# Values of an attention kernel on four quarters of TensorE's array, three score tiles, gathers a step further ahead

## The chip, the cores and the metric

The kernel runs on one core of one Trainium2 chip. The metric is the device time of one execution in microseconds (us). Three executions of the kernel before took 1350.11, 1344.72 and 1342.0 us; their median is 1344.72.

## The reference

Talking-heads attention for 4 batches, 12 heads, 448 positions and 64 channels per head, and behind it two MLPs (768 to 2048 to 768) on all 1792 tokens:

```python
scores = np.matmul(q, k.transpose(0, 1, 3, 2)) / np.sqrt(64)
scores = np.einsum('bhij,hg->bgij', scores, w_pre)      # mixes the heads ("pre mix")
attn = softmax(scores)                                  # over j, with 1e-9 in the divisor
attn = np.einsum('bhij,hg->bgij', attn, w_post)         # mixes the heads again ("post mix")
x = np.matmul(attn, v)                                  # values; then tokens x 768
h = x @ moe_w_in;   x = np.where(h > 0, h, np.exp(np.minimum(h, 0)) - 1) @ moe_w_out
h = x @ moe2_w_in;  out = np.maximum(h, 0) ** 2 @ moe2_w_out
```

## The kernel before, in words

The diff touches the attention stage and the plan that starts the MLPs beside its end; the MLPs themselves (from about 436 us on) keep their order.

**Tiling.** The 448 rows of a batch are cut into groups of 10 rows, and the groups into four chunks of 12, 11, 11 and 11 groups. There are 16 chunks (4 batches) and 180 groups. Two groups make a step: T = 90 steps. In memory a partition of a score tile holds one pair of (row of a group, head), so that one matmul can mix heads.

**The stages.** `scores(n, p)` (L141 to L151) makes the scores of heads p and p + 6 of chunk n in two PSUM banks; it uses four quarters (64 x 64) of the array at once, and there are six such pairs per chunk. `keep_scores` copies the banks to the chunk's score tile `sc[n]`. `gather(s)` (L161 to L168) fetches the 120 lines of each of the two groups of step s from the score tile to a tile `graw`, with two DMAs per group, so four per step. `mix_pre(s)` mixes heads (L176), `maxima(s)` finds the maxima on VectorE (L184) and the exponentials on ScalarE (L186), `weigh(s)` makes the weights with the divisor, `mix_post(s)` (L210) mixes again and turns the tile, `keep_weighed` (L225; L222 and L223 in the last steps) copies the result to `at[n]`. `values(n, i)` (L229 to L242) multiplies by v for two heads: each matmul contracts 112 positions and fills 64 output channels, so it uses one half of the array, and two run beside each other. Six such calls make a chunk; the first three fill one "pv" bank, the last three fill it again. `keep_x` (L247) copies a full bank, `store_x` (L254) stores it to DRAM two steps later.

**The order.** It is written out by hand: each engine and each queue works in program order. In step s the loop at its end issues weigh(s + 1), at most one pair of scores, gather(s + AHEAD) with AHEAD = 4, mix_pre and maxima of step s + 2, the stores, mix_post(s), the values of the step, further scores, keep_x, and then loads. `put` fills the table of what is done beside which step: pairs of scores of chunk n between the last gather of chunk n - 2 and the first of chunk n (two score tiles take turns), query loads four steps before, values in the five steps behind a chunk's last group, the step with the fewest scores taking two. All DMAs of the stage go through the sync queue (SP) but a few at the very start: gathers, key tiles `kt` (L120), query tiles `qt` (L129), values `v` (L136), stores `xd` (L254), and near the end tokens for the first MLP, `tmp` (L620), and weights (L407, L503). Of `graw` there are eight tiles, so a gather can be issued when the pre mix of four steps before is done.

**PSUM and the end.** Of the eight banks three are "qk" (scores), two "mix", two "post" and one "pv". `Mlps.plan` closes the pools of keys, queries and one score tile at step `last` (`start`) and opens the pools `xp` and `tp` in their space; `load_x` fills `tmp` tiles in `tp`, `split_x` splits them.

Of the kernel before, what the change touches and what calls it, by code (L numbers as in the profile page):

```python
# [45 lines left out]
BANKS = {"qk": 3, "mix": 2, "post": 2, "pv": 1}  # L46
# [6 lines left out]
def attention(tc, dram, psum, qr, kr, vr, w_pre, w_post, diagonal, xd, mlps):  # L53
# [6 lines left out]
    with ExitStack() as ctx:  # L60
        work = ctx.enter_context(tc.tile_pool(name="work", bufs=1, side="left"))
        score_ctx = [ctx.enter_context(ExitStack()) for _ in range(2)]
# [4 lines left out]
        AHEAD, MIX, LATE = 4, 2, 2  # L67
# [71 lines left out]
        sc, taken, weighed, summed, stored = {}, [], [], [], []  # L139

        def scores(n, p, tags=("qk", "qk")):  # L141

            if p == 0:
                sc[n] = score[(n + 1) % 2].tile([128, H, S], F32, name="sc", bufs=1)
            k = kt[chunks[n][0]]
            out = [bank(psum, tag)[:, :S] for tag in tags]
            for c, (x, y) in enumerate(QROWS):
                for a in range(2):
                    o = slice(64 * a, 64 * a + 64)
                    nc.tensor.matmul(out[a][64 * c : 64 * c + 64], qt[n][o, p, x:y], k[o, p, :], start=True, stop=True)  # L150
            taken.extend((sc[n][:, 6 * a + p, :], out[a]) for a in range(2))  # L151
# [9 lines left out]
        def gather(s):  # L161
            for t in (2 * s, 2 * s + 1):
                n, g = groups[t]
                x = work.tile([128, S], F32, name="graw", bufs=2 * (AHEAD - MIX + 2))
                for r in range(2):
                    lines = slice(SROWS[r] + g, SROWS[r] + g + (R5 - 1) * H + 1, H)
                    nc.sync.dma_start(out=x[64 * r : 64 * r + HALF], in_=sc[n][lines])
                graw[t] = x  # L168
# [10 lines left out]
        def maxima(s):  # L179
            tot[s] = work.tile([128, 2], F32, name="tot", bufs=3)  # L180
            ex[s] = []
            for r, p in enumerate(mixed.pop(s)):
                nmax = work.tile([128, 1], F32, name="nmax", bufs=4)
                nc.vector.tensor_reduce(nmax, p, AX.X, ALU.max, negate=True)  # L184
                e = work.tile([128, S], F32, name="ex", bufs=2 * (MIX + 2))
                nc.scalar.activation(e, p, AF.Exp, bias=nmax, scale=1.0, accum_out=tot[s][:, r : r + 1])  # L186
                ex[s].append(e)
# [40 lines left out]
        def values(n, i):  # L228
# [3 lines left out]
            if i % 3 == 0:  # L232
                pv[n] = bank(psum, "post" if n == N - 1 and i else "pv")[:, : 3 * CH].rearrange("p (k i) -> p k i", k=3)
            for jc in range(JC):
                for g in (2 * i, 2 * i + 1):
                    o = 64 * (g % 2)
                    nc.tensor.matmul(  # L237
                        pv[n][o : o + 64, i % 3, :w], vt[b, i // 3][:, jc, g % 6 * D : (g % 6 + 1) * D], at[n][:, jc, g, :w],
                        start=(jc == 0), stop=(jc == JC - 1),
                    )  # L240
            if i % 3 == 2:
                summed.append((xd[b][:, i - 2 : i + 1, r0 : r0 + w], pv[n][:, :, :w]))  # L242

        def keep_x(s):
            for o, p in summed:
                x = work.tile([128, 3, CH], F32, name="xs", bufs=3)[:, :, : o.shape[2]]
                nc.scalar.copy(x, p)  # L247
                stored.append((s + LATE, o, x))
            summed.clear()
# [12 lines left out]
        work_at = [0] * (T + 8)  # L262
# [10 lines left out]
        for n in range(N):  # L273
# [3 lines left out]
            steps = sorted(steps + [min(steps, key=lambda x: work_at[x])])  # L277
# [9 lines left out]
        idle = work.tile([128, 512], mybir.dt.bfloat16, name="idle", tag="ex", bufs=2 * (MIX + 2))  # L287
# [7 lines left out]
        tags = ("qk", "qk"), ("mix", "mix"), ("post", "post"), ("qk", "pv")  # L295
# [7 lines left out]
        load_q(1, 0, 4)  # L303
        load_mixes()
        load_q(1, 4, 6)
        for n in range(2):
            for p in range(4 if n else 6):
                scores(n, p, tags[(6 * n + p) % 4] if n == 0 else ("qk", "qk"))
                keep_scores((act, dve))
                if n and p % 2:  # L310
                    mix_pre(p // 2)
                    maxima(p // 2)
            if n == 0:
                prepare_mixes()
                for s in range(AHEAD):
                    gather(s)
        weigh(0)
        for p in range(2):
            put(p, scores, 1, 4 + p)
# [30 lines left out]
        keep_x(T)  # L350
# [188 lines left out]
class Mlps:  # L539
# [474 lines left out]
```

## Time and profile before

| | us |
|---|---|
| median of three runs | 1344.72 |
| the profiled execution | 1345.77 |
| its span, first to last instruction | 1344.0 |
| TensorE busy in the span | 1301.3 (97%) |
| VectorE, ScalarE busy | 939.0 (70%), 687.1 (51%) |
| attention stage, to the first matmul of the MLPs | about 436 |

The sums below are made on the profiled execution, whose span lies 1.8 us under its own time. Matmuls are pipelined, and one that waits for its operand counts as busy, so a busy TensorE need not be one at its peak. The sync queue has no busy share on the page: it issues only, and what it does is read from its timeline.

### The profile page before, as it was taken

How to read it: one execution, taken by the hardware profiler on the slowest of the kernel's cores; microseconds unless marked ns; L12 is line 12 of the kernel's file. 1: busy time of each engine (PE TensorE's matmuls, PEld its weight loads, DVE VectorE, ACT ScalarE, POOL GpSimd, SP SyncE). 2: the span in 40 equal slices, each digit the busy share in tenths (PEclk: the TensorE clock that was granted, in tenths of full speed). 3: DMA queues.
4: the chain of work that ended last, by engine and by line, in shares of the span. 5: the costliest groups of instructions: out<-in, count | busy, mean ns of one | idle time of the engine just before them, and what ended most of it. 6: DMA issues, size and time to landing. Idle time of an engine off the chain costs nothing.

```text
span 1344.0 us, 33493 instructions
## 1 busy us (share of the span) xinstructions
PE 1301.3 (97%) x13456; PEld 1105.0 (82%) x13456; DVE 939.0 (70%) x1944; ACT 687.1 (51%) x1478; POOL 48.8 (4%) x110
## 2 busy tenths in 40 slices
PE   7899999999999999999989999999999999999998
PEld 3556566556567999998889999999999998999998
DVE  4556556547474899877789998767885548887452
ACT  4456556546563677433344454546664535445342
POOL 0001000001022000000000000000000000000000
PEclk9999999989999999999989999999999999999999
DMA  4544544554453555465666654513122120222131
GB/s 136 161 158 152 168 151 145 167 156 153 166 176 113 184 177 165 149 186 175 199 226 218 213 198 142 182 61 97 50 65 72 54 70 25 71 65 71 42 100 41
DMA packets 121662, 178.14 MB, mean 133 GB/s; under 512 B 24259, under 2 KB 99875, under 8 KB 121507
## 3 DMA queue, kind: packets, MB, share of 16 engines
q1 hardware_dynamic: 121266, 175.71, 41.0%
q8 instruction: 106, 1.74, 0.5%
q14 instruction: 50, 0.40, 0.1%
q10 hardware_dynamic: 240, 0.29, 0.1%
HBM read 101.07 MB, written 36.18 MB: 102 GB/s over the span
## 4 chain that ended last, share of the span: by engine, by line
PE 77%; DMA 11%; DVE 6%; ACT 3%; SPq 2%; issue 1%; POOL 0%; ACTq 0%; POOLq 0%
DMA graw<-sc 8%; PE ps_qk L635 8%; PE ps_qk L636 8%; PE ps_qk L637 8%; PE ps_mix L176 5%; PE ps_post L635 5%; PE ps_post L637 5%; PE ps_post L636 5%; PE ps_post L210 5%; PE ps_mix L637 5%; PE ps_mix L636 5%; PE ps_mix L635 5%; PE ps_qk L150 4%; PE ps_pv L237 4%; PE ps_pv L636 2%; PE ps_pv L637 2%
## 5 line engine op out<-in xcount | busy, mean ns | idle before, releaser
L490 ACT CAST wh<-wf 128x384 fp32r<-128x384 f32 (+1 forms) x272 | 133.2, 491 | 214.5 <-DVE wf L449 129.8
L497 DVE TENSOR_TENSOR wl<-wf,wh 128x384 fp32r<-128x384 f32 (+1 forms) x272 | 143.5, 530 | 78.9 <-ACT wh L490 77.2
L184 DVE TENSOR_REDUCE nmax<-ps_mix 128x1 f32<-128x448 f32 x180 | 106.2, 620 | 128.1 <-PE ps_mix L176 126.0
L176 PE MATMUL ps_mix<-graw,pre 60*64 60x448 f32 x720 | 144.1, 558 | 17.0 <-DMA graw<-sc 12.9
L186 ACT ACTIVATE ex<-ps_mix,nmax 128x448 f32<-128x448 f32 x180 | 112.9, 632 | 91.9 <-DVE nmax L184 91.0
L210 PEld LDWEIGHTS ps_post<-wg,ex 60*48 60x48 f32 (+1 forms) x5760 | 116.2, 129 | 33.6 <-issue 30.5
L641 DVE TENSOR_TENSOR rl<-hr,rh 128x896 fp32r<-128x896 f32 x96 | 104.5, 1089 | 54.1 <-ACT rh L640 54.1
L155 ACT COPY sc<-ps_qk 128x448 f32<-128x448 f32 x179 | 87.0, 539 | 88.1 <-PE ps_qk L150 34.0
L150 PE MATMUL ps_qk<-kt,qt 64*64 64x448 f32 x740 | 111.4, 572 | 12.1 <-ACT sc L155 8.6
L210 PE MATMUL ps_post<-wg,ex 60*64 60x60 f32 (+1 forms) x5760 | 119.1, 219 | 0.2 <-issue 0.2
L640 ACT CAST rh<-hr 128x896 fp32r<-128x896 f32 x96 | 90.0, 938 | 50.3 <-PE ps_post L637 25.1
L176 PEld LDWEIGHTS ps_mix<-graw,pre 60*64 60x64 f32 x720 | 40.5, 136 | 87.2 <-DMA graw<-sc 39.1
L225 DVE COPY at<-ps_post 112x480 f32<-112x480 f32 x174 | 105.7, 649 | 6.9 <-PE ps_post L210 6.8
L237 PE MATMUL ps_pv<-at,v 112*64 112x110 f32 (+2 forms) x1488 | 89.6, 267 | 0.0
L419 ACT ACTIVATE wf<-wd 128x384 f32<-128x384 f32 (+1 forms) x134 | 68.0, 512 | 38.6 <-DMA wd<-w1o 23.4
L635 PE MATMUL ps_qk<-xh,wh 128*128 128x448 f32 x216 | 79.3, 367 | 0.0
L636 PE MATMUL ps_qk<-xl,wh 128*128 128x448 f32 x216 | 79.0, 366 | 0.0
L637 PE MATMUL ps_qk<-xh,wl 128*128 128x448 f32 x216 | 78.9, 365 | 0.0
L237 PEld LDWEIGHTS ps_pv<-at,v 112*64 112x64 f32 x1488 | 73.2, 138 | 5.4 <-issue 0.3
L449 DVE SCALAR_TENSOR_TENSOR wf<-wd,wf 128x384 int32<-128x384 int32 (+1 forms) x134 | 67.7, 509 | 3.9
L447 DVE SCALAR_TENSOR_TENSOR wf<-wd,wf 128x384 int32<-128x384 int32 (+1 forms) x134 | 67.7, 509 | 3.8
L150 PEld LDWEIGHTS ps_qk<-kt,qt 64*64 64x64 f32 x740 | 26.7, 134 | 45.6 <-ACT sc L155 28.6
(242 smaller groups left out, 3043.2 us busy)
## 6 DMA issues: line engine op xcount, KB each, us to landing
graw<-sc SPq DMA_DIRECT2D x360, 105.0 KB
wd<-w1i SPq DMA_DIRECT2D x32, 384.0 KB
wd<-w1o SPq DMA_DIRECT2D x48, 256.0 KB
wd<-w2i SPq DMA_DIRECT2D x32, 384.0 KB
wf<-w2of SPq DMA_DIRECT2D x48, 192.0 KB
wd<-w2o SPq DMA_DIRECT2D x22, 384.0 KB
w1if<-wf SPq DMA_DIRECT2D x32, 192.0 KB
w1of<-wf SPq DMA_DIRECT2D x48, 128.0 KB
```

The lines of the kernel that those rows point to most:

```text
L150: nc.tensor.matmul(out[a][64 * c : 64 * c + 64], qt[n][o, p, x:y], k[o, p, :], start=True, stop=True)
L176: nc.tensor.matmul(out[r][64 * g : 64 * g + 64], pre64[o], e[g][o], start=True, stop=True)
L184: nc.vector.tensor_reduce(nmax, p, AX.X, ALU.max, negate=True)
L186: nc.scalar.activation(e, p, AF.Exp, bias=nmax, scale=1.0, accum_out=tot[s][:, r : r + 1])
L210: nc.tensor.matmul(out[g][x:y, c, r], e[o, c * NJ + x : c * NJ + y], w[o, r], start=True, stop=True)
L225: nc.vector.tensor_copy(o, p)
L237: nc.tensor.matmul(pv[n][o : o + 64, i % 3, :w], vt[b, i // 3][:, jc, g % 6 * D : (g % 6 + 1) * D], at[n][:, jc, g, :w], start=(jc == 0), ...
L490: self.nc.scalar.copy(hi, f)
L497: self.nc.vector.tensor_tensor(lo, self.single.pop(i), hi.bitcast(F32), ALU.subtract)
L635: mm(p, wh, xh, start=first, stop=False)
L636: mm(p, wh, xl, start=False, stop=False)
L637: mm(p, wl, xh, start=False, stop=last)
```

## The change

Four things: PSUM and values, the score tiles and their order, the distance of gathers and query loads, and the start.

- `values` splits each contraction of 112 positions in 64 and 48. The two parts use different rows of the array and fill two "pv" banks, so four matmuls of 64 x 64 quarters stand where two of 112 x 64 stood. `keep_x` copies the first bank on ScalarE; the new `add_x` adds the second on VectorE and hands the sum to the store. "qk" has two banks in place of three, "pv" two in place of one.
- Three score tiles take turns. The 84 pairs of scores of chunks 2 to 15 are spread evenly over the first 79 steps. In a step the last pair comes behind the values, and its copies at the start of the next step, as does keep_x; add_x comes behind the copies of mix_post.
- AHEAD is 5; `graw` still has eight tiles, `ex` six in place of eight. A query load stands nine steps ahead of its first scores.
- At the start the loads of query tile 1 come behind the first gather, all scores of chunk 1 before the first step, and twelve matmuls on an idle tile between chunk 0 and chunk 1.
- At the end `start` closes two score tiles, `split_x` is a step later, and the MLPs take the four tags in turn (two banks each).

```diff
-BANKS = {"qk": 3, "mix": 2, "post": 2, "pv": 1}
+BANKS = {"qk": 2, "mix": 2, "post": 2, "pv": 2}
...
-        score_ctx = [ctx.enter_context(ExitStack()) for _ in range(2)]
+        score_ctx = [ctx.enter_context(ExitStack()) for _ in range(3)]
...
-        AHEAD, MIX, LATE = 4, 2, 2
+        AHEAD, MIX, LATE = 5, 2, 2
...
-                sc[n] = score[(n + 1) % 2].tile([128, H, S], F32, name="sc", bufs=1)
+                sc[n] = score[n % 3].tile([128, H, S], F32, name="sc", bufs=1)
...
-                x = work.tile([128, S], F32, name="graw", bufs=2 * (AHEAD - MIX + 2))
+                x = work.tile([128, S], F32, name="graw", bufs=2 * (AHEAD - MIX + 1))
...
-                e = work.tile([128, S], F32, name="ex", bufs=2 * (MIX + 2))
+                e = work.tile([128, S], F32, name="ex", bufs=2 * (MIX + 1))
...
-                pv[n] = bank(psum, "post" if n == N - 1 and i else "pv")[:, : 3 * CH].rearrange("p (k i) -> p k i", k=3)
+                tag = "post" if n == N - 1 and i else "pv"
+                pv[n] = [bank(psum, tag)[:, : 3 * CH].rearrange("p (k i) -> p k i", k=3) for _ in range(2)]
             for jc in range(JC):
-                for g in (2 * i, 2 * i + 1):
-                    o = 64 * (g % 2)
-                    nc.tensor.matmul(
-                        pv[n][o : o + 64, i % 3, :w], vt[b, i // 3][:, jc, g % 6 * D : (g % 6 + 1) * D], at[n][:, jc, g, :w],
-                        start=(jc == 0), stop=(jc == JC - 1),
-                    )
+                for r, (x, y) in enumerate(((0, 64), (64, NJ))):
+                    for g in (2 * i, 2 * i + 1):
+                        o = 64 * (g % 2)
+                        nc.tensor.matmul(
+                            pv[n][r][o : o + 64, i % 3, :w], vt[b, i // 3][x:y, jc, g % 6 * D : (g % 6 + 1) * D],
+                            at[n][x:y, jc, g, :w], start=(jc == 0), stop=(jc == JC - 1),
+                        )
...
-                nc.scalar.copy(x, p)
+                nc.scalar.copy(x, p[0])
+                adding.append((o, x, p[1]))
+            summed.clear()
+
+        def add_x(s):
+            for o, x, p in adding:
+                nc.vector.tensor_tensor(x, x, p, ALU.add)
                 stored.append((s + LATE, o, x))
-            summed.clear()
+            adding.clear()
...
-        for n in range(2, N):
-            start = (first[n - 1] - 1) // 2 - AHEAD + 1
-            steps = first[n] // 2 - AHEAD - start
-            for p in range(6):
-                put(start + p * steps // 6, scores, n, p)
-                work_at[start + p * steps // 6] += 1
-            put(start - 4, load_q, n)
+        pairs = [(n, p) for n in range(2, N) for p in range(6)]
+        steps = first[-2] // 2 - AHEAD
+        scored = [i * steps // len(pairs) for i in range(len(pairs))]
+        for x, (n, p) in zip(scored, pairs):
+            put(x, scores, n, p)
+            if p == 0 and n > 2:
+                put(x - 9, load_q, n)
...
+        for p in range(6):
+            scores(0, p, tags[p % 4])
+            keep_scores((act, dve))
+        prepare_mixes()
+        gather(0)
+        load_q(1)
+        for s in range(1, AHEAD):
+            gather(s)
+        load_q(2)
+        fill(12)
+        for p in range(6):
+            if p in (0, 2):
+                mix_pre(p // 2)
+                maxima(p // 2)
+            scores(1, p, ("qk", "qk"))
+            keep_scores((act, dve))
         weigh(0)
...
+            keep_scores()
+            keep_x(s)
             if s + 1 < T:
                 weigh(s + 1)
-            for a in pairs[:1]:
-                scores(*a)
-                keep_scores()
             if s + AHEAD < T:
                 gather(s + AHEAD)
...
                 keep_weighed(s > T - 4)
+            add_x(s)
+            for a in pairs[:-1]:
+                scores(*a)
+                keep_scores()
             for f, a in beside:
                 if f is values:
                     f(*a)
-            for a in pairs[1:]:
+            for a in pairs[-1:]:
                 scores(*a)
-                keep_scores()
-            keep_x(s)
...
-        return bank(self.psum, ("qk", "mix", "post", "pv", "qk", "mix", "post", "qk")[self.banks % 8])
+        return bank(self.psum, ("qk", "mix", "post", "pv")[self.banks % 4])
...
             early_ctx.close()
+            score_ctx[2].close()
             score_ctx[1].close()
...
-            put(last + 2 + i // 2, self.split_x, i)
+            put(last + 3 + i // 2, self.split_x, i)
```

## Rows read from the trace of the kernel before

**Rows 1.** The page's engine totals: busy us (share of the span), instructions.
```profile
PE 1301.3 (97%) x13456; PEld 1105.0 (82%) x13456; DVE 939.0 (70%) x1944; ACT 687.1 (51%) x1478; POOL 48.8 (4%) x110
```
**Rows 2.** Windows: stretch, length, busy us per engine (count), clock, DMA share, GB/s.
```profile
27.10:409.60 382.50, 358.36 (x8244) 228.69 (x8240) 226.06 (x525) 211.91 (x554) 40.74 (x93) 0.98 0.50 159
```
**Rows 3.** Timeline of the sync queue: start, us, queue, line, operation, tiles, count.
```profile
12.43 1.18 SPq L129 DMA_DIRECT2D qt<-qr  x2
13.72 15.98 SPq L167 DMA_DIRECT2D graw<-sc  x20
...
370.95 12.39 SPq L167 DMA_DIRECT2D graw<-sc  x12
...
383.92 0.96 SPq L620 DMA_DIRECT2D tmp<-xd  x2
...
406.02 3.45 SPq L167 DMA_DIRECT2D graw<-sc  x4
```
**Rows 4.** The queue's issues by line, 13.6 to 409.6 us: ns min/median/max.
```profile
L167 SPq DMA_DIRECT2D graw<-sc x360: 720/737/952, 13.7 to 408.8; - x180
...
L136 SPq DMA_DIRECT2D v<-vr x32: 322/474/1762, 31.1 to 351.2; - x32
...
L129 SPq DMA_DIRECT2D qt<-qr x29: 514/594/1505, 13.0 to 345.3; - x29
L254 SPq DMA_DIRECT2D xd<-xs x28: 365/420/697, 72.4 to 409.6; - x28
...
L120 SPq DMA_DIRECT2D kt<-kr x18: 466/567/674, 61.7 to 274.9; - x18
```
**Rows 5.** Waits of the sync queue, 13.6 to 409.6 us: total us, times, longest.
```profile
SPq L167 <- PE ps_mix L176: 20.1, 39, 0.9
SPq L167 <- DMA graw<-sc: 15.4, 37, 1.0
...
SPq L167 <- ACT sc L155: 3.3, 2, 2.2
```
**Rows 6.** Timeline of TensorE: a steady step, and a step with two value groups.
```profile
303.68 0.98 PE L150 MATMUL ps_qk<-kt,qt 64*64 64x448 f32 x8
304.48 0.93 PE L176 MATMUL ps_mix<-graw,pre 60*64 60x448 f32 x8
305.24 1.09 PE L210 MATMUL ps_post<-wg,ex 60*64 60x60 f32 x64
306.26 0.97 PE L237 MATMUL ps_pv<-at,v 112*64 112x110 f32 x16
307.16 0.98 PE L150 MATMUL ps_qk<-kt,qt 64*64 64x448 f32 x8
...
312.89 1.73 PE L237 MATMUL ps_pv<-at,v 112*64 112x110 f32 x32
314.55 0.98 PE L150 MATMUL ps_qk<-kt,qt 64*64 64x448 f32 x8
```
**Rows 7.** Timeline of VectorE: the last score copy of chunk 0, and the steady step.
```profile
12.42 0.62 DVE L155 COPY sc<-ps_mix 128x448 f32<-128x448 f32 x1
...
306.55 1.21 DVE L225 COPY at<-ps_post 112x480 f32<-112x480 f32 x2
```
**Rows 8.** Groups of instructions: busy us, mean ns, idle before, what ended it.
```profile
L247 ACT COPY xs<-ps_pv 128x330 f32<-128x330 f32 (+2 forms) x28 | 12.5, 445 | 8.3 <-PE ps_pv L237 8.3
...
L497 DVE TENSOR_TENSOR wl<-wf,wh 128x384 fp32r<-128x384 f32 (+1 forms) x272 | 143.5, 530 | 78.9 <-ACT wh L490 77.2
```
**Rows 9.** Timelines of TensorE and ScalarE at the end of the attention stage.
```profile
415.75 0.54 PE L176 MATMUL ps_mix<-graw,pre 60*64 60x448 f32 x1
...
432.02 2.39 PE L237 MATMUL ps_post<-at,v 112*64 112x108 f32 x48
...
434.83 0.55 ACT L419 ACTIVATE wf<-wd 128x384 f32<-128x384 f32 x1
...
437.87 0.48 PE L637 MATMUL ps_mix<-xh,wl 128*128 128x448 f32 x1 [1.37 <-DVE wl L497]
```

More of the change, by code (lines that the diff above doesn't have):

```diff
@@ L136, in load_v @@
             nc.sync.dma_start(out=vt[b, i][:, c, :], in_=vr[b][:, at : at + DM // 2])
-        sc, taken, weighed, summed, stored = {}, [], [], [], []
+        sc, taken, weighed, summed, adding, stored = {}, [], [], [], [], []
         def scores(n, p, tags=("qk", "qk")):
             if p == 0:
-                sc[n] = score[(n + 1) % 2].tile([128, H, S], F32, name="sc", bufs=1)
+                sc[n] = score[n % 3].tile([128, H, S], F32, name="sc", bufs=1)
             k = kt[chunks[n][0]]
@@ L232, in values @@
             if i % 3 == 0:
-                pv[n] = bank(psum, "post" if n == N - 1 and i else "pv")[:, : 3 * CH].rearrange("p (k i) -> p k i", k=3)
+                tag = "post" if n == N - 1 and i else "pv"
+                pv[n] = [bank(psum, tag)[:, : 3 * CH].rearrange("p (k i) -> p k i", k=3) for _ in range(2)]
             for jc in range(JC):
-                for g in (2 * i, 2 * i + 1):
-                    o = 64 * (g % 2)
-                    nc.tensor.matmul(
-                        pv[n][o : o + 64, i % 3, :w], vt[b, i // 3][:, jc, g % 6 * D : (g % 6 + 1) * D], at[n][:, jc, g, :w],
-                        start=(jc == 0), stop=(jc == JC - 1),
-                    )
+                for r, (x, y) in enumerate(((0, 64), (64, NJ))):
[5 more added lines that the diff above has]
+                        )
             if i % 3 == 2:
-                summed.append((xd[b][:, i - 2 : i + 1, r0 : r0 + w], pv[n][:, :, :w]))
+                summed.append((xd[b][:, i - 2 : i + 1, r0 : r0 + w], [p[:, :, :w] for p in pv[n]]))
         def keep_x(s):
@@ L260, in put @@
             extra.setdefault(max(0, s), []).append((f, a))
-        work_at = [0] * (T + 8)
-        for n in range(2, N):
-            start = (first[n - 1] - 1) // 2 - AHEAD + 1
-            steps = first[n] // 2 - AHEAD - start
-            for p in range(6):
-                put(start + p * steps // 6, scores, n, p)
-                work_at[start + p * steps // 6] += 1
-            put(start - 4, load_q, n)
+        pairs = [(n, p) for n in range(2, N) for p in range(6)]
[5 more added lines that the diff above has]
+                put(x - 9, load_q, n)
         for b in range(1, B):
@@ L276, in attention @@
             steps = [start + i for i in range(5)] if n < N - 1 else [T] * 5
-            steps = sorted(steps + [min(steps, key=lambda x: work_at[x])])
+            steps = sorted(steps + [min(steps, key=scored.count)])
             for i, x in enumerate(steps):
@@ L284, in attention @@
         mlps.plan(put, T, first[-2] // 2 - AHEAD, work, early_ctx, score_ctx)
-        idle = work.tile([128, 512], mybir.dt.bfloat16, name="idle", tag="ex", bufs=2 * (MIX + 2))
+        idle = work.tile([128, 512], mybir.dt.bfloat16, name="idle", tag="ex", bufs=2 * (MIX + 1))
         nc.gpsimd.memset(idle, 0.0)
@@ L294, in attention @@
         act, dve = nc.scalar.copy, nc.vector.tensor_copy
-        tags = ("qk", "qk"), ("mix", "mix"), ("post", "post"), ("qk", "pv")
+        tags = ("qk", "qk"), ("mix", "mix"), ("post", "post"), ("pv", "pv")
         two = nc.sync, nc.scalar
@@ L302, in attention, with fill @@
         load_k(0, 4, 6)
-        load_q(1, 0, 4)
         load_mixes()
[L305 to L316, printed above, removed]
+        def fill(n):
+            p = bank(psum, "mix")
+            for _ in range(n):
+                nc.tensor.matmul(p, idle[:, :128], idle, start=True, stop=True)
+        for p in range(6):
[14 more added lines that the diff above has]
+            keep_scores((act, dve))
         weigh(0)
-        for p in range(2):
-            put(p, scores, 1, 4 + p)
         for s in range(T + 3):
@@ L349, in attention @@
                 f(*a)
-        keep_x(T)
         store_x(T + LATE + 3)
```

## The prediction

> **What bounds the kernel now.** I began with the engine totals: TensorE is busy for 97% of the span [rows 1], which suggests that anything taken off it is gained. The windows then split the span: the change touches only the attention stage, up to about 436 us, and there TensorE's time is stretched by waiting matmuls while the DMA engines stand at 0.50 [rows 2]. The view that decides is the timeline of the sync queue (SP), which issues every load, gather and store. From its first gather at 13.72 us to the end of its last (406.02 + 3.45 = 409.47) the rows follow each other almost without a gap; twenty gathers in 15.98 us are 0.80 us each [rows 3].
>
> That queue can be added up. Issues by their medians [rows 4]: 360 gathers x 0.737 = 265.3, 32 value loads x 0.474 = 15.2, 28 query loads x 0.594 = 16.6, 28 stores x 0.420 = 11.8, 18 key loads x 0.567 = 10.2, and fourteen small ones, about 6: 325 us. Between two issues lie 0.80 - 0.74 = 0.06 us, 480 times: 30. So 355 of the 395.7 us are issuing. Waits for the landing of an earlier transfer take 15.4 us in the largest row and with the small ones of the same view 21.5 [rows 5]. The 19 us left are issues longer than their median and waits for compute engines. The row that blames the mixing matmuls for 20.1 us in 39 waits [rows 5] I do not believe: gathers take 0.720 to 0.952 us each [rows 4], which leaves no room for half a microsecond of waiting; it names releases that fell into an issue. Real are the 3.3 us for score copies [rows 5], and one shows as twelve gathers that took 12.39 us instead of 9.6 [rows 3].
>
> So the queue hardly ever waits for compute, and TensorE waits for the queue. **The attention stage ends when the queue has issued its last gather, plus a tail.** What the change does to TensorE counts only if it moves one of these two.
>
> **The change, part by part.** The sum stands against the profiled execution, 1345.77 us for a span of 1344.0; the median of the three runs, 1344.72, is 1.05 lower.
>
> *Values on four quarters.* A steady step takes 3.48 us on TensorE: scores 0.80, pre mix 0.76, post mix 1.02, values 0.90 [rows 6]. Two groups of values in a row take 1.66, so a further group costs 0.76 [rows 6]: 0.90 - 0.76 = 0.14 is lost after a group, and before it post mix with 1.02 against some 0.91 of its own (1.09 less the 0.18 by which each row overlaps the next) loses 0.11. Four quarters move the same columns in the same time (scores already run so: eight instructions of one pair in 0.80), so 0.25 in each of 76 steps with values goes: 19 us of TensorE's time. All of it is hidden by the queue; if the queue were faster it would be gained. The Trainium skill, TensorEngine Tiling, Key Properties, says that a change of tiling mode drains the engine; the losses on both sides of the values agree, and if TensorE set the pace the sum would be 19 us lower by it.
>
> *Two banks, added.* Both "pv" banks belong to one half chunk, and VectorE frees the second with add_x, behind the two at-copies. In a steady step these end at 306.55 + 1.21 = 307.76 [rows 7]; the add is near 0.46 (330/384 of the 0.530 of a tensor_tensor on 384 columns, against 0.445 for ACT's copy [rows 8]). Values that open a half chunk one step after the half before it start at 308.2, not 306.26: 2.0 us of standing TensorE. By the lists of steps in the code that meets 20 openings (15 in mid chunk, 5 at a new chunk): 40 us, 2.5 per chunk. Behind it wait that step's last score pair and the next pre mix. TensorE needs per chunk 6 x 0.80 + 5.6 x (0.76 + 0.91) + 6 x 0.76 = 18.7 us, with the stall 21.2; the queue needs 395.7 / 16 = 24.7. Covered by 3.5 us per chunk: 0. VectorE, busy for 226 of 382 us of the stage [rows 2], has room for the adds.
>
> *Three score tiles, scores spread evenly and last in a step.* The queue's waits for score copies go. Bounds: -3.3 and, if the whole rest of 19 us were compute, -19. I take -5: the 3.3 and little more, since the median issues leave no sign of longer waits. What is late next is the landing.
>
> *AHEAD 5 with the same eight gather tiles.* A gather still waits for the pre mix four steps earlier, so the queue cannot run further ahead; the other entries only come later against the gathers. Gathers, loads and stores up to the last gather are as many as before. Landing waits: 0, bounds +5 (a key load and a query load now meet in one step) and -21.5.
>
> *Prologue.* Query tile 1 moves behind the first gather. Two of its four issues, 1.18 us, lay between the last score copy (12.42 + 0.62 = 13.04) and the first gather at 13.72 [rows 3, 7]: -0.6. Its two issues now stand among the gathers: 2 x 0.594 = +1.2.
>
> *MLP plan.* At `start` the pools of two score tiles are closed, the third among them, whose last reader is that step's gather. load_x reuses the space; if its first tile lies there, the queue waits for that gather to land. Before, it went out at 383.92, right behind twelve gathers and a store [rows 3]. Bounds: 0, and one landing, at most the 6.3 from the last issue at 409.47 to the last pre mix matmul at 415.75 [rows 3, 9]. I take the middle, +3.
>
> *Tail.* After the last landing TensorE runs without gaps: values of chunk 14 now meet the 2.0 us stall once more (+2.0), three drains before values go (-0.3). At the start of the MLPs ACT sized a weight (434.83) behind the last copy of values, and TensorE waited for the halves until 437.87 [rows 9]; that copy now comes a step later, behind the sizing: about -2 of the 3.5 us after 434.41. Together 0, bounds +2 and -2. The bank rotation afterwards still takes eight banks in turn: 0.
>
> Sum: -5 - 0.6 + 1.2 + 3 = -1.4, so 1344.4 beside the profile and **1343** beside the median.
>
> **The rivals.**
> *As forecast* (0.63): within about 9 us of 1343, 1334 to 1352, from the bounds of -5, +3 and the tail.
> *Faster: landings* (0.22). The waits of 21.5 us for landings lie around query and key loads. If spreading the queries lets gathers land sooner, three quarters go: -16, 1327; all of it 1322. For it: DMA engines half idle. Against: the same transfers through the same queue, no deeper buffer. The Trainium skill's DMA page (DMA: Bandwidth & Descriptors, Issuing engines are not separate DMA queues) speaks for it: it calls the time to initiate a DMA usually small beside the DMA, by which landings would set the pace; rows 3 and 4 disagree, 355 us of issues against 21.5 of landing.
> *Slower: values behind the add* (0.10). It decides once the stalls exceed 24.7 - 18.7 = 6.0 us per chunk, 4.8 each at 20 openings. At 6 each (stall plus a late score pair and a late pre mix) TensorE needs 18.7 + 7.5 = 26.2: 1.5 x 16 = +24, 1367. For it: nothing else can free that bank. Against: 2.0 by the rows. The Trainium skill, TensorEngine Tiling, Gotcha 1: PSUM Pressure, warns of this side of the change: row tiles write to different banks, so more banks are held at once; no run here shows the price.
> *The quarters do not run together* (0.05). Values then take 6 x 0.76 = 4.6 more per chunk, 25.8 with the stall: +1.1 x 16 = +18, 1361. Against: scores and mixes do.
>
> **How the numbers follow.** About 1%, 13.4 us, is what a measurement of this kernel can tell from no change. Faster than 1331: nearly all of the landing case, 0.22. Slower than 1358: the last two, 0.13 rounded. Between: 0.65. The range reaches down to 1320, a little beyond the end of the landing case, and up to 1357, the forecast's own bounds (+5 for landings on top of 1352); the two slow cases and a rest of the fast one, 0.2 together, lie outside.
>
> **What would show it.** Right: the sync queue again has no gaps, the first gather near 13.1 and the last near 405 to 408, gathers of 0.737 us; TensorE's wait at pre mix for gathers grows by about what the drains saved; values after post mix without the 0.11; "pv" matmuls waiting for VectorE some 2 us, twenty times. Wrong: a last gather before 395 (landing waits gone or compute waits that I took for issues), or queue gaps that end at the pre mix (TensorE too slow).

## The result and the profile after

The changed kernel took 1351.03 us (median of 11, 1345.17 to 1354.56), the kernel before 1342.4 beside it (11 runs, 1340.33 to 1350.11): a ratio of 1.0051 [1.0031, 1.0072]. Forecast were 1343 and no change. The time is inside the range, but the kernel got slower by 0.5% where the sum said a tenth of a per cent faster. The profiled execution of after took 1346.93 us, near the fast end of its runs, so its trace shows less of the loss than the median does.

Windows of after, the columns as in [rows 2]; TensorE's totals of its page, as in [rows 1]:

```profile
27.10:409.60 382.50, 325.70 (x9651) 250.78 (x9648) 239.90 (x562) 214.51 (x558) 41.89 (x95) 0.98 0.50 160
```

```profile
PE 1268.7 (94%) x15004; PEld 1126.0 (84%) x15004; DVE 953.7 (71%) x1978; ACT 687.2 (51%) x1476; POOL 49.2 (4%) x110
```

TensorE is busy 33 us less in the stage than in [rows 2] (between the same two times, 27.1 and 409.6 us), and the stage does not get shorter. The sync queue of after, timeline as in [rows 3], and its waits as in [rows 5] (13.3 to 409.4 us):

```profile
385.13 0.81 SPq L634 DMA_DIRECT2D tmp<-xd  x2
...
406.13 3.26 SPq L167 DMA_DIRECT2D graw<-sc  x4
```

```profile
SPq L167 <- DMA graw<-sc: 19.3, 43, 1.2
SPq L167 <- PE ps_mix L176: 17.3, 37, 0.9
...
SPq L634 <- DMA graw<-sc: 4.0, 2, 3.2
...
SPq L167 <- ACT sc L155: 1.2, 2, 0.7
```

The last gather ends at 409.39 us (409.47 before). Waits for ScalarE's score copies fell by 2.1 us, waits for landings rose by 3.9, and load_x (L634) waits 4.0. Behind the last gather stands the tail. TensorE there, with the wait ahead of a row and what ended it in brackets:

```profile
415.78 0.54 PE L176 MATMUL ps_mix<-graw,pre 60*64 60x448 f32 x1
416.16 0.92 PE L210 MATMUL ps_post<-wg,ex 60*48 60x60 f32 x50
...
418.67 0.97 PE L239 MATMUL ps_pv<-at,v 48*64 48x110 f32 x28 [1.40 <-DVE tot L191]
...
437.24 0.47 PE L651 MATMUL ps_mix<-xh,wl 128*128 128x448 f32 x1
```

and the groups of the values line with what ended TensorE's idle time before them (us, times; idle time of its weight loads is counted in):

```profile
L239 PE MATMUL ps_pv<-at,v x2976: 251/254/424, 60.4 to 433.2; 64*64 64x110 f32 x54, 48*64 48x110 f32 x48, 64*64 64x120 f32 x26, 48*64 48x120 f32 x25
...
  issue: 50.8, 40
  DVE tot L191: 29.1, 17
  DVE xs L255: 5.5, 5
```

The last mix starts where it did [rows 9], and the second half of chunk 14's values then waits 1.40 us for VectorE's add (the trace names its neighbour, L191). The MLPs' first low-half product (L651) starts 0.63 us earlier than in [rows 9] all the same: what this execution lost, 1.2 us, it lost behind that point.

### The profile page after: what moved, and what is told of

The parts are those of the page before. It is cut to its first block, busy times and chain, and to the rows that moved or that the text cites. A ratio compares the mean times of both kernels' runs of the same rounds, so it can differ in the third digit from the quotient of the medians.

```text
span 1345.2 us, 36691 instructions
## 1 busy us (share of the span) xinstructions
PE 1268.7 (94%) x15004; PEld 1126.0 (84%) x15004; DVE 953.7 (71%) x1978; ACT 687.2 (51%) x1476; POOL 49.2 (4%) x110
## 3 DMA queue, kind: packets, MB, share of 16 engines
q8 instruction: 118, 1.93, 0.6%
## 4 chain that ended last, share of the span: by engine, by line
PE 75%; DVE 10%; DMA 8%; ACT 3%; issue 2%; SPq 1%; POOL 0%; ACTq 0%; DVEq 0%; POOLq 0%
DMA graw<-sc 5%; PE ps_qk L649 5%; PE ps_qk L650 5%; PE ps_qk L651 5%; PE ps_post L210 5%; PE ps_mix L176 5%; PE ps_post L649 5%; PE ps_post L651 5%; PE ps_post L650 5%; PE ps_pv L650 5%; PE ps_mix L649 5%; PE ps_mix L651 5%; PE ps_mix L650 5%; PE ps_qk L150 5%; PE ps_pv L239 5%; PE ps_pv L651 5%
## 5 line engine op out<-in xcount | busy, mean ns | idle before, releaser
L503 ACT CAST wh<-wf 128x384 fp32r<-128x384 f32 (+1 forms) x272 | 133.5, 493 | 208.0 <-DVE wf L462 128.3
L510 DVE TENSOR_TENSOR wl<-wf,wh 128x384 fp32r<-128x384 f32 (+1 forms) x272 | 144.9, 535 | 77.6 <-ACT wh L503 75.0
L210 PEld LDWEIGHTS ps_post<-wg,ex 60*48 60x48 f32 (+1 forms) x5760 | 125.4, 128 | 25.1 <-issue 13.2
L176 PE MATMUL ps_mix<-graw,pre 60*64 60x448 f32 x720 | 132.6, 561 | 13.5 <-DMA graw<-sc 9.9
L239 PE MATMUL ps_pv<-at,v 48*64 48x110 f32 (+5 forms) x2976 | 104.2, 260 | 39.5 <-DVE tot L191 29.1
L210 PE MATMUL ps_post<-wg,ex 60*48 60x60 f32 (+1 forms) x5760 | 122.9, 219 | 2.5 <-issue 1.6
L239 PEld LDWEIGHTS ps_pv<-at,v 48*64 48x64 f32 (+1 forms) x2976 | 85.7, 134 | 46.6 <-issue 43.9
L176 PEld LDWEIGHTS ps_mix<-graw,pre 60*64 60x64 f32 x720 | 53.2, 137 | 58.7 <-DMA graw<-sc 28.4
L669 ACT ACTIVATE tmp<-tmp 128x448 f32<-128x448 f32 x48 | 27.9, 581 | 56.8 <-DVE tmp L779 43.7
L649 PE MATMUL ps_qk<-xh,wh 128*128 128x448 f32 x150 | 55.4, 370 | 0.7 <-DVE tmp L676 0.7
L650 PE MATMUL ps_qk<-xl,wh 128*128 128x448 f32 x150 | 55.0, 367 | 0.0
L651 PE MATMUL ps_qk<-xh,wl 128*128 128x448 f32 x150 | 55.0, 367 | 0.0
```

The lines of the kernel that those rows point to most:

```text
L176: nc.tensor.matmul(out[r][64 * g : 64 * g + 64], pre64[o], e[g][o], start=True, stop=True)
L210: nc.tensor.matmul(out[g][x:y, c, r], e[o, c * NJ + x : c * NJ + y], w[o, r], start=True, stop=True)
L239: nc.tensor.matmul(pv[n][r][o : o + 64, i % 3, :w], vt[b, i // 3][x:y, jc, g % 6 * D : (g % 6 + 1) * D], at[n][x:y, jc, g, :w], start=(jc ...
L503: self.nc.scalar.copy(hi, f)
L510: self.nc.vector.tensor_tensor(lo, self.single.pop(i), hi.bitcast(F32), ALU.subtract)
L649: mm(p, wh, xh, start=first, stop=False)
```

## The experiments

All ratios are to the kernel before, run beside it on the same chip. The runs are spread over six chips, so kernels from different chips are compared by their ratios. The edits are excerpts; `...` stands for code left out.

| run | median us (runs) | ratio [95%] |
|---|---|---|
| a0_after_again | 1351.65 (12) | 1.0022 [0.9997, 1.0047] |
| e1_load_x_later | 1350.44 (12) | 1.0030 [1.0007, 1.0053] |
| e2_values_on_halves | 1344.66 (12) | 0.9994 [0.9970, 1.0017] |
| e3_quarters_alone | 1351.59 (12) | 1.0036 [1.0015, 1.0057] |
| rb_before_loads_elsewhere | 1345.38 (10) | 1.0009 [0.9992, 1.0026] |
| ra_after_loads_elsewhere | 1350.82 (9) | 1.0050 [1.0032, 1.0067] |
| re_halves_loads_elsewhere | 1348.98 (10) | 1.0025 [1.0007, 1.0043] |
| rt_tail_on_halves | 1345.54 (12) | 1.0009 [0.9993, 1.0024] |
| rte_tail_on_halves_load_x_later | 1344.59 (12) | 0.9992 [0.9974, 1.0011] |
| fl_tail_filled | 1357.74 (6) | 1.0102 [1.0076, 1.0128] |
| ae_add_before_part_lo | 1348.32 (12) | 1.0013 [0.9997, 1.0028] |
| aee_add_before_part_lo_load_x_later | 1345.57 (12) | 0.9988 [0.9970, 1.0006] |
| rg_gathers_on_two_queues | 1343.28 (10) | 0.9982 [0.9955, 1.0010] |
| rge_two_queues_add_before_part_lo | 1336.77 (7) | 0.9921 [0.9888, 0.9954] |
| rgx_two_queues_add_in_its_step | 1308.06 (6) | 0.9715 [0.9681, 0.9748] |
| rh_two_queues_halves | 1295.33 (5) | 0.9651 [0.9632, 0.9671] |
| ri_halves_more_matmuls | 1327.70 (6) | 0.9866 [0.9840, 0.9892] |
| rhb_before_two_queues | 1322.04 (5) | 0.9812 [0.9783, 0.9841] |

### One part of the change at a time

a0 is the changed kernel again. e1 moves the loads of the first MLP block:

```diff
-            put(last + i // 2, self.load_x, i)
-            put(last + 3 + i // 2, self.split_x, i)
+            put(last + 2 + i // 2, self.load_x, i)
+            put(last + 4 + i // 2, self.split_x, i)
```

e2 is after with `values` and `keep_x` of before and no `add_x`; e3 is before with those three of after and its banks:

```diff
e2:  -                for r, (x, y) in enumerate(((0, 64), (64, NJ))):
     +                pv[n][o : o + 64, i % 3, :w], vt[b, i // 3][:, jc, ...], at[n][:, jc, g, :w],
     -            add_x(s)
e3:  +BANKS = {"qk": 2, "mix": 2, "post": 2, "pv": 2}
                  keep_x(s)
     +            add_x(s)
```

> The changed kernel once more, unaltered, for a second profile. Theory Q (the sync queue's issues and landings set the pace): 3 to 9 us over the kernel before; the queue again without gaps that end at a compute engine, last gather issued by 405 to 415 us, landing waits 25 to 35 us (21.5 before), one wait of about 4 us in front of the first token load. Rival V (TensorE's wait for add_x sets the pace): the same time, but the queue waits for pre mix (graw tiles not free) for 10 us or more in sum.

> The changed kernel with load_x and split_x two steps (split_x one) later, so that the gather of the closed score tile has landed when the first token tile is loaded. Q: the waits of 3.2 + 0.8 us in front of the first load go, the last gather is issued some 4 us earlier, and the kernel is about 4 us faster than the changed one, 1 to 4 us over the kernel before. V: no change against the changed kernel.

> The changed kernel with values as before: 112 positions on half of the array, one bank, no add_x. TensorE loses 19 us to drains again, and its waits for add_x (some 35 us in the profile of the changed kernel) are gone. Q: within 3 us of the changed kernel, at most 2 faster (the one stall behind the last gather). V: 15 to 35 us faster than the changed kernel.

> The kernel before with only the values changed: four quarters, two pv banks (qk two), add_x right behind keep_x at the end of the step, so that the next values hardly wait for it. TensorE saves 19 us of drains and waits for nothing new. Q: within 2 us of the kernel before. Rival T (TensorE's own work sets the pace): 10 to 19 us faster than before.

Without quarters the rest of the change is worth nothing (e2), and quarters alone cost 0.36% (e3): the loss goes with the quarters. (The second measurement of the changed kernel by itself, a0, meets e2's interval; the first, 1.0051 [1.0031, 1.0072], does not.) Rivals V (e2 faster by 15 us or more) and T (e3 faster by 10 or more) fell. Theory Q missed too: e2 is 7.0 us faster than a0 where it allowed 2, e3 4.0 us slower than before where it allowed 2. In e1 the last gather ends at 404.87 instead of 408.43 us (a0), but the kernel does not end earlier. Its TensorE and VectorE behind the last gathers:

```profile
413.88 0.41 PE L239 MATMUL ps_pv<-at,v 64*64 64x110 f32 x4 [0.94 <-ACT xs L249]
418.30 1.01 PE L239 MATMUL ps_pv<-at,v 48*64 48x110 f32 x16 [4.01 <-DVE tot L191]
```

```profile
413.11 2.00 DVE L510 TENSOR_TENSOR wl<-wf,wh 128x384 fp32r<-128x384 f32 x2 [3.14 <-ACT wh L503]
...
415.73 1.14 DVE L184 TENSOR_REDUCE nmax<-ps_mix 128x1 f32<-128x448 f32 x2
416.78 0.96 DVE L222 COPY at<-ps_post 112x360 f32<-112x360 f32 x2
417.66 0.49 DVE L255 TENSOR_TENSOR xs<-xs,ps_pv 128x330 f32<-128x330 f32 x1
```

The add (L255) is issued one step after its values. Ahead of it on VectorE stand two subtractions of `part_lo` (L510), which prepare weights for the MLPs, the next step's maxima and the at-copies: the values wait 4.01 us, and no gather is left to hide it. `part_lo` waits itself, for a cast on ScalarE (L503): 3.14 us here, 0.74 in after and a0, and all that VectorE has queued behind it waits with it.

### The tail

rt puts the last two chunks' values back on halves, rte adds e1's edit; fl puts matmuls that nobody reads ahead of the mix; ae and aee (with e1's edit) issue the add ahead of part_lo.

```diff
rt:  +            rows = ((0, NJ),) if n > N - 3 else ((0, 64), (64, NJ))
fl:  +            if T - 9 < s < T - 3:
     +                for _ in range(4):
     +                    nc.tensor.matmul(p, pre64[:HALF], vt[B - 1, 1][:HALF, 0, :], start=True, stop=True)
ae:  +            if s > T - 6:
     +                keep_x(s)
     +                add_x(s)
                  for f, a in beside:
                      if f not in (scores, values):
```

> The changed kernel, with the values of the last two chunks alone on halves, as before (one bank, no add): those are the values that stand behind the last gathers, where no queue hides TensorE. Theory E (the 4 to 5 us that the quarters cost are the wait for the add and the lower granted clock behind the last gathers): 4 to 5 us below the changed kernel, at 1346 to 1347 where that is 1351.5, and within 0.1% of before. Rival M (they are in the last stage, whose matmuls start 200.0 or 206.7 ns apart for whole stretches at the same granted clock, and where this run falls is a draw that the quarters ahead of it tilt): no change, 1350 to 1352, and a profile in which the time from the last mix to the first matmul of the last stage is 20 us as before while whole stretches are 206.7 ns apart.

> The changed kernel with the last two chunks' values on halves (1345.5 us alone) and the loads of the first block of the last stage two steps later (the last gather ended 4 us earlier with that alone, but the tail behind it took 27 us where it had been 21). Theory E: with the tail of before (20 us from the last mix to the last stage) the 4 us stay won: about 1341 to 1342 us, 0.2 to 0.3% under before. Rival: the last gathers and the last stage's first operands swap places, the tail gets longer by the same 4 us: 1345 to 1346.

> The changed kernel, with four matmuls of 384 columns ahead of the mix in each of the steps T-8 to T-4 (about 375 to 410 us), whose result nobody reads: TensorE has work while it waits for the last gathers. Theory C (of the 4 to 5 us of the quarters' tail, some 3.5 are the granted clock that falls to 0.5 behind the last gathers in some executions, and 1 the wait for the add): no 0.5 between 412 and 440 us, 20 to 21.5 us from the last mix to the first matmul of the last stage, 1347 to 1349 us. Rival A (it is the wait for the add, and the clock has little to do with it): 1350 to 1353, as the changed kernel or slower by the filling's 4 us where it isn't hidden.

> The changed kernel; in the last steps (from T-5 on) the copy and the add of the values are issued at the end of their own step, ahead of part_lo, not in the step behind. Theory P (the place of the add on VectorE, behind part_lo's 2.2 us, the next maxima and copies, is what the quarters cost): TensorE no longer waits ahead of the second half of chunk 13's values, 19.5 to 20 us from the last mix to the first matmul of the last stage, 4 to 5 us below the changed kernel, at 1345 to 1347 and within 0.15% of before. Rival R (the quarters cost it elsewhere, in the time of their matmuls or in the last stage): 1350 to 1352 with that wait gone.

> The same, with the loads of the last stage's first block two steps later. Theory P: the 4 us that this won ahead of the tail stay won: 1341 to 1343, 0.2 to 0.4% under before. Rival R: 1346 to 1350.

(What these call chunk 13 is chunk 14, the last but one.) With e1's edit: late add 1.0030 [1.0007, 1.0053]; add in its own step 0.9988 [0.9970, 1.0006], apart from it; tail on halves 0.9992 [0.9974, 1.0011], whose interval just touches it. Without that edit, rt and ae lie in the same direction; their intervals are apart from that of the first measurement of the changed kernel (from 1.0031), but meet that of a0. Theories E and P of rte and aee forecast 0.2 to 0.4% under before and got 0.1: behind the add another wait shows, for an at-copy of ScalarE (L223), 1.54 us in aee and 2.45 in rte. In aee the add stands at 410.36 us and nothing waits for it:

```profile
409.19 1.22 DVE L225 COPY at<-ps_post 112x480 f32<-112x480 f32 x2 [0.42 <-PE ps_post L210]
410.36 0.50 DVE L255 TENSOR_TENSOR xs<-xs,ps_pv 128x330 f32<-128x330 f32 x1
413.13 2.01 DVE L513 TENSOR_TENSOR wl<-wf,wh 128x384 fp32r<-128x384 f32 x2 [2.27 <-ACT wh L506]
```

Theory C's forecast fell: filled, the same wait is 4.14 us long and the kernel slower than unfilled. But the filling does not price the clock, because the granted clock fell to 1.2 GHz all the same (for 6.8 us from 421 us on, behind that wait). The clock has a part in the tail: a0's granted clock has a mean of 0.60 from 412 to 424 us (at 1.2 instead of 2.4 GHz from 414 us on, for 10.2 us), where after's profile has 1.00. Windows of a0, then of after:

```profile
412.00:424.00 12.00, 10.09 (x113) 6.90 (x111) 5.13 (x11) 3.83 (x11) 4.89 (x6) 0.60 0.35 110
```

```profile
412.00:424.00 12.00, 9.11 (x216) 6.53 (x213) 6.54 (x14) 5.09 (x15) 5.53 (x6) 1.00 0.47 140
```

TensorE in a0:

```profile
413.31 2.10 PE L176 MATMUL ps_mix<-graw,pre 60*64 60x448 f32 x5 [0.55 <-DMA graw<-sc]
...
415.20 0.95 PE L176 MATMUL ps_mix<-graw,pre 60*64 60x448 f32 x1
...
419.16 1.73 PE L239 MATMUL ps_pv<-at,v 48*64 48x110 f32 x28 [1.30 <-DVE tot L191]
...
440.19 0.47 PE L651 MATMUL ps_mix<-xh,wl 128*128 128x448 f32 x1
```

From the last mix to L651 a0 takes 24.99 us, after 21.46, before 22.12. Its matmuls are slow ahead of the add already (five mixes in 2.10 us), behind waits for ScalarE and for a gather of 0.80 and 0.55 us, much as in after (0.75 for the gather); why the clock fell in the one and not in the other, these runs don't tell. In e1, fl, ra and rg 3.4 to 6.8 us at 1.2 GHz lie within the wait for the add or behind it.

### What paces the stage

In rb (on before), ra (on after) and re (on e2) the loads of keys, queries and values leave the sync queue; in rg (on after) and rhb (on before) every second gather does.

```diff
rb, ra, re:  load_k, load_q, load_v: nc.sync -> nc.gpsimd (behind the first gather)
rg, rhb:
-                    nc.sync.dma_start(out=x[64 * r : 64 * r + HALF], in_=sc[n][lines])
+                    (nc.sync, nc.gpsimd)[r if s > 5 else 0].dma_start(out=x[64 * r : 64 * r + HALF], in_=sc[n][lines])
```

> The kernel before, but the loads of keys, queries and values behind the first gather (some 76 issues, about 50 us of the sync queue's time) are issued on the GpSimd queue. Theory Q (the sync queue paces the stage from first to last gather): the stretch from the first gather to the end of the last one shortens until the next limit, which for this kernel is TensorE (358 us busy of 382 between 27 and 409 us): by 15 to 25 us, to about 1323 us. Rival L (what paces it is how fast transfers land, whatever queue issues them): the landing waits grow by what the issues shrink, within 5 us of before.

> The changed kernel with the same loads issued on the GpSimd queue. Theory Q: TensorE has only 325 us of work in the stage now, so the stretch shortens by 30 to 45 us, to about 1312 us, and is 10 to 20 us shorter than in the kernel before with the same edit: what the quarters save on TensorE shows only where the queue no longer covers it. Rival V (the add on VectorE and its wait cost the stage as much as the drains gave back): no faster than the kernel before with the same edit. Rival L: within 5 us of the changed kernel.

> The changed kernel with values on halves, as before (112 rows, one bank, no add), and the same loads issued on the GpSimd queue. Theory Q: the TensorE limit of the kernel before again, some 19 us of drains more than the changed kernel with this edit, so 10 to 20 us above it and within 6 us of the kernel before with this edit. Rival V: as fast as the changed kernel with this edit, or faster. Rival L: within 5 us of the kernel before as it was.

> The changed kernel, with every second gather (the lower 60 rows; from step 1 of the loop on) issued on the GpSimd queue, 150 to 170 transfers in all. With only the loads moved, the sync queue's busy time fell by 36 to 48 us and its waits for the transfer issued 8 before grew by as much, at the same 155 to 159 GB/s. Theory L1 (at most 8 transfers of one queue are under way, and with 7 to 8 us each that is a transfer per us; a second queue brings 8 more): the waits go and the stretch of gathers shortens by 20 to 40 us until TensorE (325 us) limits it, about 1320 us. Theory L2 (all transfers together land no faster, whatever queue they are on): the stretch stays at 390 to 400 us and the landing takes longer by what the queues issue sooner, 1345 to 1355 us. Rival G (GpSimd's waits for VectorE in the weighing hold its gathers back): the stretch gets longer by 5 us or more.

Rival L it was, in rb, ra and re: as fast as their kernels were, within 5 us. Waits of rb's sync queue (27 to 409 us), beside the 15.4 us of [rows 5]:

```profile
SPq L167 <- DMA graw<-sc: 59.7, 96, 2.3
```

Summed over the queue from the first gather to the last, its issues fell from 337.5 to 290.1 us, and 44 us of waits for landings came. Every gap of over 0.1 us that a transfer ends, 151 in rb and 71 in before, is ended by the one issued 8 before on this queue. So what I had added up as issuing was never the limit by itself: at most 8 transfers under way, of 5.8 us (median of before) to 7.1 us (rb) each, were.

The eight is in the program. In its semaphore records the sync queue's transfers take eight semaphores in turn (100, 101, 103 to 108) to tell that they landed, and each issue waits until the semaphore that it takes itself has been told of the transfer before it. GpSimd's transfers have eight others (111 to 118). So a second queue here is eight more transfers under way as well, and no run tells which of the two counts.

With gathers on two queues (rg) the landing waits go (2.7 us of them from 27 to 350 us), and the next limit shows; the last gather ends at 400.65 us, 8 us earlier and not the 20 to 40 of theory L1. TensorE's waits in rg, 27 to 350 us:

```profile
PE ps_pv L239 <- DVE tot L191: 24.0, 14, 1.8
PE ps_pv L239 <- issue: 5.9, 9, 2.3
```

The values wait for the late add all through the stage: the prediction's slow rival, with 1.7 us each, now uncovered.

### Behind two queues

rge is rg with ae's and e1's edits; rgx the same with the add at the end of its own step in all steps; rh is rgx with values on halves (e2's edit); ri is rh with eight one-column matmuls more behind each pair of heads, read by nobody.

```diff
rgx: +            keep_x(s)
     +            add_x(s)
                  for f, a in beside:
                      if f not in (scores, values):
ri:  +            for k in range(2 * JC):
     +                o, g, jc = 64 * (k % 2), 2 * i + k % 2, k // 2
     +                nc.tensor.matmul(spare[n][o : o + 64, 480:481], vt[b, i // 3][:, jc, ...], at[n][:, jc, g, :1],
     +                                 start=True, stop=True)
```

> The changed kernel with every second gather on the GpSimd queue, the add at the end of its own step from T-5 on, and the loads of the last stage's first block two steps later. With the second queue alone the last gather ended at 401 us, 8 us earlier, TensorE stood still for 2 us in the tail, and the run of the profile took 1350, the median 1343. Theory P: the tail's 3 to 4 us come off that and the loads' 4 as well: 1335 to 1339, 0.5 to 0.8% under before. Rival R: 1342 to 1345.

> The same, with the add at the end of its own step in all steps. Behind two queues TensorE's waits in the stage were for VectorE, 28 us in 16 waits ahead of values. Theory P: most of these 28 us go too, and the stretch of gathers shortens by 10 to 20 us more: 1320 to 1330. Rival W (VectorE then waits for the values at the end of a step, and its maxima come later by as much): within 3 us of the kernel with the add moved in the last steps alone, or slower.

> The kernel with gathers on two queues, the copy at the end of its own step and the later loads, with the values on halves as before (112 rows, one bank, no add). With quarters it took 1308 us, the gathers ending at 362 us with TensorE busy 311 of 343 us. Theory S (the quarters' saving on TensorE, 358 against 325 us in the stage, was there all along, hidden first by the queue and then by the add's place): TensorE at the same busy share makes the stretch of gathers 25 to 35 us longer, 1335 to 1342. Rival N (the quarters have no part in it): 1305 to 1312.

> The two-queue kernel with values on halves (1295 us), and behind each pair of heads eight more matmuls of one column into a spare column of the same bank, read by nobody: as many instructions on TensorE as with quarters, without the quarters, their second bank and their add. Theory I (TensorE waits for its instructions, by their number): the waits that nothing ends come back at distances of multiples of 126, 10 to 25 us of them in the stage, and with some 3 to 10 us of the matmuls' own the time is 1305 to 1315. Rival A (the add and the quarters are what makes them): no more than 2 us of such waits, 1297 to 1304.

> The kernel before with every second gather on the GpSimd queue and nothing else: its own steps, two score tiles, gathers 4 steps ahead, halves. Theory K (the in-flight limit of one queue was all that held the stage; the rest of the change adds nothing): 1295 to 1305 and TensorE busy over 97% of the stage. Rival D (the gathers further ahead and the third score tile are what lets the second queue run ahead): the stage is 15 us shorter at most, 1330 to 1340, with TensorE's waits for gathers and scores in it.

The add's place is worth 28.7 us here (rge to rgx, on one chip), more than theory P's 10 to 20. Then Theory S fell, and rival N missed as well: rh, without quarters, is another 0.64% faster than rgx by the ratios (8.6 us; 12.7 between the medians, from two chips), and at 1295.33 us the fastest of all. TensorE's window and waits, 27 to 350 us, of rgx, then of rh:

```profile
27.00:350.00 323.00, 294.80 (x9206) 227.12 (x9203) 228.87 (x536) 204.59 (x533) 127.88 (x245) 0.99 0.63 179
```

```profile
PE ps_pv L239 <- issue: 11.5, 12, 1.8
PE ps_post L210 <- issue: 8.1, 15, 1.3
```

```profile
27.00:350.00 323.00, 312.89 (x8160) 211.35 (x8160) 220.88 (x524) 207.57 (x545) 132.32 (x252) 0.99 0.66 184
```

```profile
PE ps_post L210 <- issue: 0.7, 1, 0.7
```

With quarters TensorE stands still for 19.6 us in waits that the views put down to nothing ("issue"); with halves for 0.7. The records of the DMA packets tell what they are: loads of instructions. From the page of rgx, packets and MB of the queue that brings them:

```profile
q8 instruction: 118, 1.93, 0.7%
```

All 27 such waits of rgx (over 0.25 us, to 392 us, 22.7 us) end 1.29 to 1.70 us behind the end of one of these 16 KiB packets. So do, within 1.20 to 1.76 us, the 10 of after, 12 of a0, 9 of e3, 12 of rg and 14 of rge, and the one each of rh and ri. rgx has 118 packets for 30,008 matmuls and weight loads, rh 106 for 26,936: about 254 each. No two of them end less than 3.3 us apart (27 to 350 us, in before, after, rgx, rh and ri), but TensorE starts 126 matmuls, about a packet's worth, within 2.46 us at the fastest in rgx, and within no less than 3.18 in before, rh and ri.

That adds up to the difference. The drains did go: from the first matmul of post mix to the first behind a group of values, undisturbed, it takes 1.93 us in before and rh and 1.75 in rgx, so 0.18 a group, 14 us for 76 groups (an estimate). The instruction waits took 22 us, and 8 us of loss are left. ri has as many matmul records as rgx (15,004) and no such wait among those from 27 to 350 us:

```profile
PE ps_qk L150 <- ACT sc L155: 3.4, 4, 1.5
PE ps_mix L176 <- DMA graw<-sc: 1.7, 3, 0.8
```

So the number alone does not make the waits: theory I had the cause, but not what brings it out, and neither its time nor rival A's came (1327.70 us). ri's records come slower: six groups of values in a row take 7.41 us in ri for 192 records, and 4.67 us in after for as many. rhb lies between K and D: the second queue alone is worth 1.9%, and the rest of the change without quarters (with the later loads and the copy in its own step) another 1.6%; with one queue, and without these two edits, it showed nothing (e2).

## Why the prediction was wrong

**The queue ends the stage:** right as long as there is one queue. TensorE lost 33 us of busy time and the last gather moved by 0.1 us. **But not by issuing.** "355 of the 395.7 us are issuing" was true as a sum and wrong as a cause (rb). The rival on landings had the right limit; it asked only whether spreading the queries would shorten the waits, and they grew. The Trainium skill, DMA: Bandwidth & Descriptors, Issuing engines are not separate DMA queues, calls the time to initiate a DMA usually small beside the transfer. I set that aside because of [rows 4]; rb agrees with the page. The page also says that a second initiating engine saves only that time; rhb, 23.7 us faster, does not settle this, since it has eight more semaphores too.

**Values, 19 us of drains saved, hidden:** hidden it was, and nearer 14 us. Six groups in a row take 4.67 us on quarters (192 records) and 4.66 on halves (96), so the same columns take the same time. "If the queue were faster it would be gained" was wrong: twice the records in the same time cost 22 us of waiting for instructions, a term that the sum does not have, and rgx is 8.6 us slower than rh by the ratios.

**Values behind the add, 40 us in 20 openings, hidden:** matmuls waited in just 20 openings of after, 32.5 us (29.1 in 17, 3.4 in 3; the other 2.1 us of the 5.5 are weight loads of the same openings), 1.6 us each, and hidden as long as one queue paced the stage.

**The tail, "together 0":** the step that failed. The forecast saw the stall for chunk 14 and priced it at 2.0 us, taken back by 2 us at the start of the MLPs; that second wait did go (L651 starts at 437.24, [rows 9] have 437.87). But the stall was priced in a steady step, behind two at-copies. In this step part_lo's subtractions, and what they wait for, stand in front of it as well: 1.4 us in after's trace, 3.65 to 4.14 in e1, fl and ra, and in a0 1.3 at a lower clock, a cost that the forecast does not have. From the last mix to L651 the tail took 0.66 us less than before in after, 2.9 us more in a0 and 5.2 more in e1, so the bounds of 2 did not hold. Its place decides: taking the add out of the way (aee against e1) is worth 0.42%, 5.7 us. How much of the changed kernel's 0.5% (0.2% in a0) the tail makes, its own two traces don't fix: in after's the loss lies behind it.

**load_x +3:** 4.0. **Score copies -5:** -2.1 by the rows. **Landings 0:** +3.9. Together the stage came out even (409.39 against 409.47 us), 1.3 us above the forecast's -1.4; what the experiments place of the loss is in the tail.

**Open:** e3 has its add at the end of its step and no wait in the tail, and yet took 0.36% more than before. Its profiled execution lost its time in the MLPs (below), which kernels with and without quarters do; whether the quarters make that likelier, these runs don't tell. re, on halves and with no add, is 0.25% slower than before as well, its last gather 3.7 us later.

## What to carry to other kernels

A queue without gaps says that the queue paces, not what paces the queue: move some of its issues away, and see whether waits for landings take their place, always for a transfer the same number of places back. Then look whether that number is one of the program's semaphores. Price a wait on an in-order engine from the step where nothing hides it, with all that is queued ahead of it there, since a cover that holds for a whole stage ends with it. A saving "hidden for now" has to be tried with the cover gone: here the cover hid a gain in the half of the change that I had priced at nothing (steps, score tiles, gathers ahead) and a loss in the half that I had priced as a gain. A wait that the views put down to nothing can still have a partner in the trace: lay it beside the instruction loads.

## What the hardware showed that I had not expected

The last stage's matmuls run in one of two rhythms, for a hundred us and more, at the same granted clock of 1.00. Windows of after, then of e3:

```profile
460.00:600.00 140.00, 140.00 (x701) 131.38 (x700) 126.88 (x301) 84.04 (x181) 0.00 (x0) 1.00 0.54 173
```

```profile
460.00:600.00 140.00, 140.00 (x679) 126.69 (x678) 123.38 (x291) 82.54 (x177) 0.00 (x0) 1.00 0.54 163
```

701 or 679 matmuls in 140 us are 200 or 206 ns each; the traces have both in kernels with quarters and with halves (rhb has 679 as well). The 18 traces of experiments have 18 (rge) to 1,794 (e3) of the MLPs' matmuls at the longer one (starts 205 to 208 ns apart); some 6.7 ns each make 0.1 to 12 us, at the upper end more than the 0.5% that this case is about.

The waits of rgx for instructions are not spread at random: each of the 26 distances between the 27 is a multiple of 126.4 matmuls within 2, about as far as a packet of instructions reaches. What the load of a packet waits for, and so what sets the 3.3 us, no run here shows.

A busy share is no load: from 27 to 350 us TensorE was busy 304 us with 7,030 matmuls in before and 313 us with 8,160 in rh. Before, it was 94% busy and could still do 16% more.
